# Ten short constant products in one tile ahead of the first hash bits, and the second pair's hash bits made by halves and signed in place

## The chip, the cores and the metric

The kernel runs on one core of a Trainium2 chip. The metric is device time in microseconds (us) of the whole program, as the median of repeated executions. A core has five engines that run their own instruction lists in order and wait for each other on semaphores: TensorE (PE in the profile, with PEld for its weight loads), VectorE (DVE), ScalarE (ACT), GpSimd (POOL) and SyncE (SP, which only issues DMAs here). ACT and POOL can issue DMAs too.

## The reference

The program computes a masked attention and then a feed-forward block on its output.

```python
# q, k, v: (4, 8, 768, 64); proj: (64, 6)
q_bits = (np.einsum('bhsd,dk->bhsk', q, proj) > 0)
k_bits = (np.einsum('bhsd,dk->bhsk', k, proj) > 0)
q_bucket = np.sum(q_bits * 2**np.arange(6), axis=-1)   # k_bucket likewise
mask = q_bucket[:, :, :, None] == k_bucket[:, :, None, :]
scores = np.where(mask, scale * q @ k.T, -1e9)
attn = softmax(scores)                                 # row maximum taken off first
x = (attn @ v) as (3072, 512)
h = x @ w_in;  g = h * erf(softplus(h));  out = g @ w_out   # w_in (512, 2048), w_out (2048, 512)
```

Six hash bits of every query and key row come from the signs of a projection; a query attends only to the keys with the same six bits.

## The kernel before, in words

**Pairs and scores.** The 32 heads are worked in 16 pairs; the two heads of a pair lie in the two halves of the 128 partitions (64 dimensions each). For a pair, q and k lie transposed as 128x768 f32. Scores are made transposed (keys on partitions, queries along the free dimension) in 12 chunks of 128 keys by 384 queries for both heads; `score(n, c)` (L550) makes one chunk, with n counting groups of three chunks, four groups per pair. A chunk is two products per head added up in PSUM: one of the f32 q and k, and one in bf16 of "bit tiles" that adds a very large negative number wherever the six bits differ. The bit tiles of a pair lie in `both[i % 2]`, a 128x2x768 bf16 tile (q in the first half, k in the second). ACT takes the exponential of every chunk (`e_all`, L568), and PE multiplies it with v (`av`, L631). DVE sums the exponentials for the divisor (L619), and PE adds them over partitions (`z_ps`, L666).

**Hash bits.** There are two ways to make them.

- By halves, in place (`hash_bits`, L373, and `take_bits`): four products of 64 output rows by 384 columns put the q bits on PSUM rows 0 to 63 and the k bits on rows 64 to 127; ACT writes the signs as bf16 straight into `both` (`sign_bits`, L386); DVE weights the k part onto both heads' partitions (`spread_bits`, L397) and copies the q part to the second head's partitions (`double_bits`, L407). The kernel before does this for pair 0 only, each half of 384 columns for itself, ahead of everything else.
- By way of DRAM (`bits_of`, L812; `sign_of`, L821; `weigh_bits`, L831; `leave_bits`, L841; `place_bits`, L850): four products of 32 output rows each, which PE runs side by side, make all bits of a pair in one 128x384 tile; ACT signs it into `sg`, DVE weights half of it, POOL sends it to DRAM (`bd`) and reads it back with two DMAs into the few rows of `both` that hold bits. The other rows must hold zeros, so each of the two `both` tiles is cleared once (a POOL memset: L433 for `both[1]` at the start, `clean`, L859, for `both[0]` after pair 0's last score). The kernel before does this for pairs 1 to 15.

**The start.** DVE sets a few constants. `WARM = 5` products of constant 128x128 and 128x256 f32 operands (L780) stand on PE ahead of pair 0's bits; each takes a new tile from a PSUM pool with one buffer (`bank`), so each waits for the one before it. Their operands lie in `w_sum`, which DVE sets first (L248). The first q and k are fetched in halves: SP issues q first half, k second half, q second half; ACT issues k first half. Then come v, pair 1, two pieces of w_in (`raw`) and pair 2, all on SP.

**What sets the order.** After the start, all steps of the attention are handed to a planner, `arrange`, as operations with an engine, an assumed cost, a rank, predecessors and a lateness; it emits them in an order, and that order is fixed per engine. PE's own order is written by hand (`order`): the scores of groups 0, 1, 2, then `bits_of(1)`, then `weigh` of groups 0 and 1, scores of groups 3 and 4, `bits_of(2)`, divisor 0, `weigh` of groups 2 and 3, and so on. Scores and bits share three PSUM buffers (`big`), so each waits for ACT to have read the one three places earlier. The first score of pair 1 is in group 4. Weights come as float64 bit patterns; POOL fetches them in pieces of 512 KB (`raw`, L456) with two buffers, and ACT and DVE turn them into f32 through the attention (L470 to L532). The feed-forward block follows on the same engines.

The lines that say how the five constant products are placed, and how the bits of pair 1 reach `both`:

```python
                nc.tensor.matmul(
                    out=bank("warm")[:, 0 : 2 * P],
                    lhsT=warm[:, 0:P],
                    rhs=warm[:, P:HS],
...
                nc.gpsimd.dma_start(out=bd.rearrange("n a r c -> (n a r) c"), in_=sg)
```

Of the kernel before, what the change touches and what calls it, by code (L numbers as in the profile page):

```python
# [63 lines left out]
P = 128  # L64
# [129 lines left out]
def kernel(  # L194
# [11 lines left out]
    nc = tc.nc  # L206
    B, H, S, D = v.shape
# [5 lines left out]
    HS = S // 2  # L213
# [15 lines left out]
    small = ctx.enter_context(tc.tile_pool(name="small", bufs=3))  # L229
    QR = 32  # L230
    QB = QR // 2
    WARM = 5
    proj_sb = const.tile([P, 2 * QR], F32, name="proj_sb")
    weight = const.tile([P, 2], F32, name="weight")
    proj_q = const.tile([P, QR], F32, name="proj_q")
# [9 lines left out]
    blocks = []  # L245
    stats = const.tile([P, 2, NPAIR, 2], F32, name="stats")
    nc.vector.memset(ones, 1.0)
    nc.vector.memset(w_sum[:, 0, 0, 0:HS], 1.0)  # L248
    warm = w_sum[:, 0, 0, 0:HS]
    proj_in = const.tile([P, 2 * NBIT], F32, name="proj_in")  # L250
    nc.gpsimd.dma_start(out=proj_in, in_=proj2)
    nc.vector.memset(proj_sb, 0.0)
# [46 lines left out]
    def bank(name):  # L299
        return misc.tile([P, 512], F32, name=name, tag="bank")  # L300
# [45 lines left out]
    def fetch(i, load, quick=False):  # L346
        d = dict(
            q=load.tile([P, S], F32, name="q", tag="q"),
            k=load.tile([P, S], F32, name="k", tag="k"),
            v=load.tile([P, NC, P], F32, name="v", tag="v"),  # L350
        )
        b, j = divmod(i, JP)
        parts = ((0, "q"), (0, "k"), (1, "k"), (1, "q")) if quick else ((None, "q"), (None, "k"))
        for half, what in parts:
            cols = slice(0, S) if half is None else slice(half * HS, half * HS + HS)
            queue = nc.scalar if quick and what == "k" and half == 0 else nc.sync
            for ab in range(2):
                queue.dma_start(
                    out=d[what][ab * D : ab * D + D, cols],
                    in_=qkT[2 * i + ab, "qk".index(what) * D : "qk".index(what) * D + D, cols],  # L360
                )
# [54 lines left out]
    def attention():  # L416
        NS = NPAIR * 4
        with (
# [11 lines left out]

            sg = bitp.tile([P, HS], BF16, name="sg")
            both = [bitp.tile([P, 2, S], BF16, name=f"both{n}") for n in range(2)]
            nc.gpsimd.memset(both[1], 0.0)  # L433
            junk = ep.tile([P, HS], BF16, name="junk")
            NE = 3 * GC
            e_all = ep.tile([P, NE, 2, HS + 1], F32, name="e_all")
# [339 lines left out]
                pairs[i] = fetch(i, load)  # L776

            pairs[0] = fetch(0, load, quick=True)
            for n in range(WARM):
                nc.tensor.matmul(  # L780
                    out=bank("warm")[:, 0 : 2 * P],
                    lhsT=warm[:, 0:P],
                    rhs=warm[:, P:HS],
                    start=True,
                    stop=True,
                )
# [11 lines left out]
            def pe(fn, args, cost, after=()):  # L798
                if chain:
                    after += (chain[-1],)  # L800
                op(fn, args, "PE", cost, (0, len(chain)), after, late=0.25)
                chain.append((fn.__name__,) + args)

            def bits_of(i):


                d = pairs[i]
                d["bits"] = big("bits")
                for n, what in enumerate("qk"):
                    for half in range(2):  # L810
                        row = (2 * n + half) * QR
                        nc.tensor.matmul(  # L812
                            out=d["bits"][row : row + QR, 0, 0:HS],
                            lhsT=proj_q,
                            rhs=d[what][:, half * HS : (half + 1) * HS],
                            start=True,
                            stop=True,
                        )
# [35 lines left out]
                        in_=bd[:, ab, 0 : NBIT + 1, :].rearrange("n r c -> r n c"),  # L854
                    )

            def clean():

                nc.gpsimd.memset(both[0], 0.0)  # L859

            chain = []
            order = [("score", 0)]
            for h in range(NH):
                order += [("score", n) for n in (2 * h + 1, 2 * h + 2) if n < NS]
                if h == 0:
                    order.insert(3, ("bits", 1))
                if h % 2 and (h + 3) // 2 < NPAIR:
                    order.append(("bits", (h + 3) // 2))
                if h >= 1:
                    order.append(("divisor", h - 1))  # L870
                order += [("weigh", 2 * h), ("weigh", 2 * h + 1)]
            slots = []
            for what, n in order:
                if what == "score":
                    i = n // 4
                    after = (("place_bits", i),)
                    if n == 0:
                        for c in range(2):
                            pe(plain, (n, c), 0.66)
                    for c in range(GC):  # L880
                        free = (slots[-3],) if len(slots) >= 3 else ()
                        pe(score, (n, c), 0.82 if n or c == 2 else 0.17, after + free)
                        slots.append(("exponential", n, c))
                elif what == "bits":
                    pe(bits_of, (n,), 0.92, (("start_pair", n), slots[-3]))
                    slots.append(("sign_of", n))
                elif what == "divisor":
                    pe(divisor, (n,), 0.42, (("sum_keys", n, last_sum(n)), ("keep_divisor", n - 1)))
                else:
                    h = n // 2  # L890
# [46 lines left out]
            for i in range(NPAIR):  # L937
                n = 4 * i
                if i:
                    op(  # L940
                        start_pair,
                        (i,),
                        "SP",
                        3.6,
                        (0, n - 6),
                        (("weigh", n - 9), ("bits_of", i - 1))
                        + tuple(("measure", i - 3, m, half) for m in range(2) for half in range(2)),
                        late=3.5,
                    )
                    op(sign_of, (i,), "ACT", 0.6, (0, n - 6, 9), (("bits_of", i), ("leave_bits", i - 1)))  # L950
                    op(weigh_bits, (i,), "DVE", 0.33, (0, n - 6, 1), (("sign_of", i),))
                    op(leave_bits, (i,), "POOL", 0.7, (0, n - 6, 2), (("weigh_bits", i),), late=2.6)
                    op(
                        place_bits,
                        (i,),
                        "POOL",
                        1.2,
                        (0, n - 6, 3),
                        (("leave_bits", i), ("score", n - 5, 2)) + (("clean",),) * (i == 2),
                        late=2.6,  # L960
                    )
                for m in range(2):
                    for half in range(2):
                        op(
                            measure,
                            (i, m, half),
                            "ACT",
                            0.5,
                            (1, 2 * i + 2, 2 + m, half),
                            (("start_pair", i), ("score", n, 0)),  # L970
                        )
                if i == NPAIR - 1:
                    continue
# [13 lines left out]
                op(normalise, (i,), "DVE", 0.95, (0, n + 8, 4), (("widen", i), ("leave", 2 * i + 1)))  # L987
                op(send, (i,), "SP", 0.35, (0, n, 4), (("normalise", i),), late=2.2)
            op(clean, (), "POOL", 1.4, (0, 0), (("score", 3, 2),), late=0.3)
            for n in range(len(pieces)):  # L990
                op(
                    fetch_weights,
# [771 lines left out]
```

## Time and profile before

| what | value |
|---|---|
| median of 17 runs | 919.82 us (918.64 to 922.63) |
| the profiled execution | 918.42 us, of which its span is 916.6 us |
| busy in the span | PE 904.6, DVE 819.7, ACT 767.9, POOL 46.5 us |
| attention, about | 10 to 320 us |
| feed-forward, about | 320 to 917 us |
| DMA | 83.05 MB, mean 91 GB/s |

The span runs from the first to the last instruction; all places below are microseconds from its start. The profiled execution is 1.8 us longer than its span, and 1.4 us shorter than the median. Busy time of PE counts a matmul from its start to its modelled end, so passes that overlap are merged. An f32 product shows as two records (two passes), a bf16 product as one. A releaser is what ended an engine's idle time.

### The profile page before, as it was taken

Reading aid. Unit: us, or ns where it says so; the run is one execution under the profiler, and the core shown is the slowest. Engines: PE = TensorE matmul, PEld = TensorE weight load, DVE = VectorE, ACT = ScalarE, POOL = GpSimd, SP = SyncE. Lnnn points to the kernel's source line nnn. Section 1 sums busy time; section 2 is a strip of 40 time slices with the busy share of each in tenths; the row PEclk is TensorE's granted clock in tenths of the full one; section 3 lists DMA queues with packets and bytes.
Section 4 is the critical chain, followed back from the end, with each engine's and each line's share of the span. In section 5 each row is a group of like instructions: output and inputs, shape, how many; then the busy total and the mean of one; then the engine's idle time right before and its main releaser. Section 6 shows DMA issues by size and latency. Waiting matters only on the chain.

```text
span 916.6 us, 13120 instructions
## 1 busy us (share of the span) xinstructions
PE 904.6 (99%) x5006; PEld 658.8 (72%) x5006; DVE 819.7 (89%) x1020; ACT 767.9 (84%) x1002; POOL 46.5 (5%) x83
## 2 busy tenths in 40 slices
PE   9999999999999999999999999999999999999997
PEld 4444444444444478888888888888888888888885
DVE  4899999999998979899999799988899889988995
ACT  5788887788887749999988998899989997899892
POOL 1211111111111000000000000000000000000000
PEclk9999999999999999999999999999999999999999
DMA  8455567655673131102022112201121121111201
GB/s 206 122 151 160 158 184 192 184 147 158 185 200 98 59 122 64 46 3 101 12 72 78 36 46 69 81 35 46 70 81 35 35 75 40 36 35 46 69 35 49
DMA packets 62966, 83.05 MB, mean 91 GB/s; under 512 B 34174, under 2 KB 47342, under 8 KB 62896
## 3 DMA queue, kind: packets, MB, share of 16 engines
q1 hardware_dynamic: 56672, 64.08, 24.2%
q0 software_dynamic: 6064, 17.86, 6.1%
q8 instruction: 41, 0.67, 0.3%
q14 instruction: 29, 0.24, 0.1%
q10 hardware_dynamic: 160, 0.20, 0.1%
HBM read 64.71 MB, written 17.40 MB: 90 GB/s over the span
## 4 chain that ended last, share of the span: by engine, by line
PE 96%; DVE 2%; ACT 1%; DMA 1%; issue 0%; POOL 0%; DVEq 0%; ACTq 0%; POOLq 0%
PE M L1323 31%; PE X L1183 28%; PE st L550 16%; PE av L631 14%; PE M L1183 3%; PE z_ps L666 1%; PE bits L812 1%; PE warm L780 1%; ACT e_all L568 1%; DVE e L1237 0%; DMA bd<-sg 0%; PE bits L373 0%; DVE h L1265 0%; DMA both<-bd 0%; DVE S L1280 0%
## 5 line engine op out<-in xcount | busy, mean ns | idle before, releaser
L1250 DVE SCALAR_TENSOR_TENSOR e<-w,e 128x1024 f32<-128x1024 f32 x144 | 173.4, 1220 | 5.8 <-ACT w L1246 3.0
L568 ACT ACTIVATE e_all<-st 128x768 f32<-128x768 f32 x192 | 151.1, 812 | 14.0 <-PE st L550 13.1
L1246 ACT ACTIVATE w<-w,cq 128x1024 f32<-128x1024 f32 x144 | 160.6, 1143 | 1.9
L550 PE MATMUL st<-q,k 64*128 64x384 f32 x768 | 155.2, 483 | 0.0
L1323 PE MATMUL M<-w_out_sb,h 128*128 128x256 f32 x576 | 140.2, 379 | 0.4 <-DVE h L1265 0.4
L631 PE MATMUL av<-e_all,v 128*64 128x385 f32 (+1 forms) x768 | 131.2, 490 | 0.0
L1183 PE MATMUL X<-x,w_in_sb 128*128 128x256 f32 x512 | 121.1, 379 | 0.0
L1323 PEld LDWEIGHTS M<-w_out_sb,h 128*128 128x128 f32 x576 | 109.3, 190 | 15.9 <-DVE h L1265 1.1
L1183 PEld LDWEIGHTS X<-x,w_in_sb 128*128 128x128 f32 x512 | 97.0, 190 | 13.8 <-ACT h L1201 0.6
L631 PEld LDWEIGHTS av<-e_all,v 128*64 128x64 f32 x768 | 52.3, 136 | 67.5 <-issue 66.6
L1323 PE MATMUL M<-wt,S 128*128 128x256 f32 x384 | 93.4, 379 | 0.4 <-DVE S L1280 0.4
L550 PEld LDWEIGHTS st<-q,k 64*128 64x128 f32 x768 | 68.3, 188 | 35.0 <-issue 34.3
L1183 PE MATMUL X<-x_sum,w_sum 128*128 128x256 f32 x344 | 81.7, 380 | 1.8 <-ACT h L1201 1.8
L1323 PEld LDWEIGHTS M<-wt,S 128*128 128x128 f32 x384 | 72.9, 190 | 10.7 <-DVE S L1280 0.8
L1183 PEld LDWEIGHTS X<-x_sum,w_sum 128*128 128x128 f32 x344 | 65.0, 190 | 12.0 <-ACT h L1201 3.3
L1201 ACT COPY h<-X 128x512 f32<-128x512 f32 x85 | 49.0, 576 | 22.3 <-PE X L1183 21.4
L1227 DVE SCALAR_TENSOR_TENSOR w<-w,e 128x1024 f32<-128x1024 f32 x48 | 58.4, 1221 | 9.7 <-ACT w L1222 9.6
L550 PE MATMUL st<-both 64*128 64x384 bf16 x384 | 63.1, 324 | 0.9 <-DMA both<-bd 0.9
L1265 DVE TENSOR_TENSOR h<-h,e 128x1024 f32<-128x1024 f32 x48 | 58.0, 1220 | 5.8 <-ACT e L1261 5.5
L1241 ACT ACTIVATE w<-e 128x1024 f32<-128x1024 f32 x48 | 50.4, 1050 | 13.3 <-DVE e L1237 13.0
L1237 DVE TENSOR_TENSOR e<-e,w 128x1024 f32<-128x1024 f32 x48 | 57.5, 1218 | 2.7 <-ACT e L1233 2.6
L1205 DVE TENSOR_TENSOR h<-X,h 128x512 f32<-128x512 f32 x65 | 44.8, 690 | 16.3 <-PE X L1183 15.4
(133 smaller groups left out, 1377.1 us busy)
## 6 DMA issues: line engine op xcount, KB each, us to landing
wt<-wt SPq DMA_DIRECT2D x24, 768.0 KB, 4.2
raw<-in_w_out_dram POOLq DMA_DIRECT2D x16, 512.0 KB, 4.0
raw<-in_w_in_dram POOLq DMA_DIRECT2D x14, 512.0 KB, 4.4
v<-in_v_dram SPq DMA_DIRECT2D x32, 192.0 KB, 4.7
xs<-x SPq DMA_DIRECT2D x16, 384.0 KB, 2.6
q<-in_qkT_dram SPq DMA_DIRECT2D x30, 192.0 KB, 4.1
k<-in_qkT_dram SPq DMA_DIRECT2D x30, 192.0 KB, 4.2
r<-rd SPq DMA_DIRECT2D x30, 192.0 KB, 3.4
```

Of the source, the lines that this page charges most:

```text
L550: nc.tensor.matmul(out=st[:, ab, 0:HS], lhsT=d["k" + src][rows, keys], rhs=d["q" + src][rows, cols], start=(part == 0), stop=(part == 1),)
L568: nc.scalar.activation(out=e[:, :, 0:HS], in_=st[:, :, 0:HS], func=AF.Exp, scale=scale)
L631: nc.tensor.matmul(out=d["av"][rows, 0:w], lhsT=d["v"][:, g * GC + c, rows], rhs=e[:, ab, 0:w], start=(g == 0 and c == 0), stop=(g == 1 an ...
L1183: nc.tensor.matmul(out=d[where][:, u, :], lhsT=a[:, kc, f : f + P], rhs=b[:, kc, :], start=(first and u == 0 and kc == 0), stop=(last and ...
L1201: nc.scalar.copy(out=quarter(p, q), in_=st[p][where])
L1227: nc.vector.scalar_tensor_tensor(out=w, in0=w, scalar=-1.0, in1=st[p]["e", v], op0=ALU.add, op1=ALU.subtract)
L1237: nc.vector.tensor_tensor(out=s, in0=s, in1=st[p].pop(("w", v)), op=ALU.subtract)
L1241: nc.scalar.activation(out=z, in_=st[p]["s", v], func=AF.Square)
L1246: nc.scalar.activation(out=q, in_=z, func=AF.Square, bias=cq[:, j : j + 1])
L1250: nc.vector.scalar_tensor_tensor(out=s, in0=st[p].pop(("q", v, j)), scalar=ERF_Q[j][1], in1=s, op0=ALU.add, op1=ALU.mult,)
L1265: nc.vector.tensor_tensor(out=h, in0=h, in1=st[p].pop(("s", v)), op=ALU.mult)
L1323: nc.tensor.matmul(out=banks[name][:, sub, :], lhsT=a[:, u, sub * P : (sub + 1) * P], rhs=b[:, u, :], start=(c == 0 and k == 0), stop=(c = ...
```

## The change

Four edits, and what they carry with them:

1. Ten constant products in place of five. All ten write one tile (`warm = bank("warm")`, taken once), rows 0 to 63, 128 columns; the weights are the 128x64 tile `ones`, the moving operand is one column of `ones` repeated 128 times. The memset of `w_sum` (L248) goes.
2. `bits_of(1)` calls `hash_bits`: four products of 64 rows by 384 columns. `place_first` (ACT) signs all 768 columns into `both[1]`, `weigh_first` (DVE, twice) and `double_first` (DVE) do the rest. `sign_of(1)`, `weigh_bits(1)`, `leave_bits(1)` and `place_bits(1)` go, and with them three DMAs on POOL. Scores of pair 1 wait for `double_first`.
3. The memset of `both[1]` at the start goes, since all of `both[1]` is now written; `clean` is there for both tiles, after the last score of pair 0 and of pair 1, ahead of pairs 2 and 3.
4. `leave_bits` and `place_bits` tell the planner a lateness of 3.6 in place of 2.6.

The order of instructions by engine differs only here. PE: the constant products and the bits of pair 1. DVE: the memset is gone; two `spread` and one `double` of 64x768 stand in the place of one 64x384 weighting; just after it, the read of `av`'s last column (`ev`) comes two instructions later, the two shifts of weight piece 1 come ahead of group 1's sums instead of after them, and the weighting of pair 2's bits one sum earlier. ACT: the sign of pair 1's bits comes one `junk` (a square with a sum) later, and one reading of a weight piece (`keep<-raw`) comes one exponential earlier. POOL: no memset at the start and no DMAs for pair 1, so `clean(0)` is first, then the weight piece; a second `clean` stands ahead of pair 3's DMAs. SP is unchanged, and so is everything after.

```diff
-    WARM = 5
+    WARM = 10
...
-    nc.vector.memset(w_sum[:, 0, 0, 0:HS], 1.0)
-    warm = w_sum[:, 0, 0, 0:HS]
...
-            nc.gpsimd.memset(both[1], 0.0)
...
+            warm = bank("warm")
             for n in range(WARM):
                 nc.tensor.matmul(
-                    out=bank("warm")[:, 0 : 2 * P],
-                    lhsT=warm[:, 0:P],
-                    rhs=warm[:, P:HS],
+                    out=warm[0:D, 0:P],
+                    lhsT=ones,
+                    rhs=ones[:, 0:1].broadcast_to([P, P]),
...
             def bits_of(i):
+                if i == 1:
+                    hash_bits(pairs[i], big)
+                    return
...
-            def clean():
-
-                nc.gpsimd.memset(both[0], 0.0)
+            def place_first():
+
+                cols = slice(0, S)
+                sign_bits(pairs[1], lambda what: both[1][:, "qk".index(what[0]), :], cols)
+
+            def weigh_first(ab):
+                spread_bits(pairs[1], slice(0, S), ab)
+
+            def double_first():
+                double_bits(pairs[1], slice(0, S))
+
+            def clean(n):
+
+                nc.gpsimd.memset(both[n], 0.0)
...
-                    after = (("place_bits", i),)
+                    after = (("double_first",) if i == 1 else ("place_bits", i),)
...
-                    pe(bits_of, (n,), 0.92, (("start_pair", n), slots[-3]))
-                    slots.append(("sign_of", n))
+                    pe(bits_of, (n,), 0.92 if n > 1 else 1.44, (("start_pair", n), slots[-3]))
+                    slots.append(("sign_of", n) if n > 1 else ("place_first",))
...
+                    if i == 1:
+                        op(place_first, (), "ACT", 0.9, (0, n - 2, 9), (("bits_of", i),))
+                        for ab in (1, 0):
+                            op(weigh_first, (ab,), "DVE", 0.43, (0, n - 2, 1), (("place_first",),))
+                        op(double_first, (), "DVE", 0.35, (0, n - 2, 2), (("weigh_first", 0), ("weigh_first", 1)))
...
-                        (("leave_bits", i), ("score", n - 5, 2)) + (("clean",),) * (i == 2),
-                        late=2.6,
+                            (("leave_bits", i), ("score", n - 5, 2), ("clean", i - 2)),
+                            late=3.6,
...
-            op(clean, (), "POOL", 1.4, (0, 0), (("score", 3, 2),), late=0.3)
+            for n in range(2):
+                op(clean, (n,), "POOL", 1.4, (0, 4 * n), (("score", 4 * n + 3, 2),), late=0.3)
```

More of the change, by code (lines that the diff above doesn't have):

```diff
@@ L865, in attention @@
                 if h == 0:
-                    order.insert(3, ("bits", 1))
+                    order.append(("bits", 1))
                 if h % 2 and (h + 3) // 2 < NPAIR:
@@ L949, in attention @@
                     )
[L950 to L958, printed above, removed]
-                        (("leave_bits", i), ("score", n - 5, 2)) + (("clean",),) * (i == 2),
-                        late=2.6,
-                    )
+                    if i == 1:
[3 more added lines that the diff above has]
+                        op(double_first, (), "DVE", 0.35, (0, n - 2, 2), (("weigh_first", 0), ("weigh_first", 1)))
+                    else:
+                        op(sign_of, (i,), "ACT", 0.6, (0, n - 6, 9), (("bits_of", i), ("leave_bits", i - 1)))
+                        op(weigh_bits, (i,), "DVE", 0.33, (0, n - 6, 1), (("sign_of", i),))
+                        op(leave_bits, (i,), "POOL", 0.7, (0, n - 6, 2), (("weigh_bits", i),), late=3.6)
+                        op(
+                            place_bits,
+                            (i,),
+                            "POOL",
+                            1.2,
+                            (0, n - 6, 3),
+                            (("leave_bits", i), ("score", n - 5, 2), ("clean", i - 2)),
+                            late=3.6,
+                        )
                 for m in range(2):
```

## The prediction

> **What bounds the kernel now.** The page first: its busy times, then its chain.
>
> ```profile
> PE 904.6 (99%) x5006; PEld 658.8 (72%) x5006; DVE 819.7 (89%) x1020; ACT 767.9 (84%) x1002; POOL 46.5 (5%) x83
> PE 96%; DVE 2%; ACT 1%; DMA 1%; issue 0%; POOL 0%; DVEq 0%; ACTq 0%; POOLq 0%
> ```
>
> TensorE sets the time almost everywhere, so a microsecond that PE gets back early is kept to the end unless another engine cannot follow. The change touches the first 50 us only, so I read the chain there, in order of time (start, duration, what):
>
> ```profile
> 1.40 1.24 PE warm L780 x2
> ...
> 7.74 2.54 PE bits L373 x8
> 10.27 1.70 PE st L550 x10
> 11.97 0.02 issue
> 11.99 5.14 ACT e_all L568 x8
> ...
> 20.24 2.72 DMA bd<-sg
> ...
> 24.21 2.15 DMA both<-bd
> 26.36 0.05 issue
> 26.40 2.59 PE st L550 x17
> 28.99 0.78 PE bits L812 x8
> ```
>
> Two things are seen. The constant products hold PE until 7.7 us. And at 20 to 26 us the chain is not PE's but runs through the two DMA hops of pair 1's bits. PE's timeline shows what that costs:
>
> ```profile
> 24.25 0.33 PE L550 MATMUL st<-both 64*128 64x384 bf16 x2
> 24.41 0.81 PE L550 MATMUL st<-q,k 64*128 64x384 f32 x4
> 25.88 0.32 PE L550 MATMUL st<-both 64*128 64x384 bf16 x1 [0.66 <-DMA both<-bd]
> 27.15 0.39 PE L550 MATMUL st<-both 64*128 64x384 bf16 x2
> ```
>
> Score chunks come every 0.80 to 0.81 us (22.62, 23.44, 24.25), so the next bit products were due at 25.06. The pair after them starts at 27.15 in place of 25.86: 1.29 us lost. For the start I read the weight loader's timeline, then SP's issues and their median from issue to landing:
>
> ```profile
> 2.67 0.50 PEld L780 LDWEIGHTS warm<-w_sum 128*128 128x128 f32 x2 [0.78 <-PE warm L780]
> 3.54 1.24 SPq L358 DMA_DIRECT2D q<-in_qkT_dram  x2
> q<-in_qkT_dram SPq DMA_DIRECT2D x4, 96.0 KB, 2.9
> ```
>
> Every constant product waits 0.78 us for the one before, at a pitch of 1.27. The last data that pair 0 needs is q's second half, whose second DMA is issued at about 4.2 (half of 1.24 after 3.54). It lands at about 6.8 to 7.1 (the k issues on ACT's queue take 2.6, these 2.9).
>
> Last, how much room DVE has in the attention (columns: stretch, length, busy PE, PEld, DVE, ACT, POOL, clock, DMA share, GB/s):
>
> ```profile
> 88.00:268.00 180.00, 180.00 (x1334) 83.60 (x1328) 171.04 (x228) 146.81 (x272) 26.02 (x46) 1.00 0.62 169
> ```
>
> PE is full, and DVE is at 95%: a second engine that can become the bound.
>
> **1. The constant products.** The `w_sum` memset goes. The first weight load stood 0.06 after that memset's end (1.34); `ones` is set at 0.93, so it now starts at 0.99. The old products took until 7.67, where bits begin. The new ones have no wait between them. Price of a pass: the 384-column f32 passes of pair 0's bits start at 7.67, 8.36, 9.00 and 9.64, 0.64 each, so 128 columns take 0.21 and twenty passes 4.3. With 0.1 for the first load PE is free at 5.4. Bounds: at the later pitch (f32 score passes, 0.32) 2.1 us; if each product kept a wait, the old pitch of 1.27 without half its columns (0.43), 0.84, times ten, 8.4. I take 4.3: these are passes in one queue without waits, as the bits are.
>
> **2. Pair 0's bits.** First half at 5.4: `proj_sb` is written by 4.3, and the first q and k land by 2.2 + 2.9 = 5.1. The second half waits for its q: 6.9 (middle of 6.8 and 7.1). Its two passes end at 7.55 with 0.32 each, where the first scores stood at 10.20: 2.65 earlier (2.45 to 2.75 by the landing). If passes still take 0.64 then, they end at 8.2. Late next is that DMA; the products no longer are. ACT's first sign took 0.58, DVE's first half 0.32 + 0.32 + 0.25. The first bit products come two chunks (1.3) after the scores' start, and the second half's DVE work is first needed by the score group after that, as before; all these shift together. ACT's exponentials follow PE from 11.99, then from 9.3.
>
> The clock. In this trace the 0.64 passes last until about 10.2, nine microseconds after the constant products began, with gaps, and two and a half after the gaps ended. The Trainium skill ("TensorE: Matmul & The Clock Gate", Part 1) states that the array runs at half rate until one window of about 3.4 us has been busy, the window running free of the kernel. By the rule ten gapless products from 1.0 release it by 7.8 at the latest, by the row alone possibly not before 9.9. The rule would leave the sum as it stands; staying slow to 9.9 is the second case below.
>
> **3. Pair 1's bits on PE.** Four 32-row products run side by side in 0.78 (the chain's last line). Two at a time at full rate take half of pair 0's 2.54: 1.27. Cost 0.49, on the path. Bounds: 0.4 to 0.6, from passes of 0.32 without and with a start gap of 0.1.
>
> **4. The way of the bits.** Gone are the sign of 0.58, the weighting of 0.32, three DMAs and two landings (2.7 and 2.2). New: ACT signs 128x768, between the 0.81 of an exponential of that size and twice 0.58; DVE runs two 64x768 weightings (0.32 to 0.64 each) and a copy (0.25 to 0.51). On the clock of before, bits end at 19.1; ACT has a `junk` pair in front (0.71) and is free at 19.85; sign to 20.7 (21.0); DVE to 22.3 (22.8). The score that needs it stands at 25.06 + 0.49 = 25.55: 2.7 us of cover at the worst. So the whole 1.29 is gained. Behind the new DVE work are two shifts of a weight piece (1.1) and, later than before, `ev` (end about 24.8); the product that waits for `ev` stands at about 29, and ACT's reading of `av` no longer waits for it. Group 1's sums start about 1.4 later than PE's pace asks; the exponentials that overwrite their input come at 35.09 before, with 4 us of cover left. What DVE is behind is made up by its own idle time (0.7 at 43.4, 0.6 at 62.4). Extra DVE work: 0.57 to 1.47 us, taken 1.2, at nothing. One cost I charge: ACT's reading of a weight piece (0.65) now stands before the third exponential of group 3, whose buffer PE wants 0.5 later: 0.15 (0 to 0.65).
>
> **5. The memsets and POOL.** The memset at 2.45 (1.40) had an idle POOL and delays nothing. `clean(0)` no longer stands behind two DMA issues (1.14) and starts with the last reading of `both[0]` (24.25 + 0.33). The weight fetch queued behind it came at 26.09; on the clock of before it now comes at about 26.9, when DVE is done with its buffer, which is 24.3 after the gain of 2.65. Landing takes 5.5, to 29.8, and ACT wants it at 35.80 - 3.3 = 32.5. `clean(1)` runs at about 46 on the old clock, between a weight fetch (43.30) and pair 3's DMA (51.82): nothing behind it waits. SP's queue is unchanged, and the fetch of pair 3 follows PE.
>
> The same memset beside DVE: `clean(0)` ran at 24.77 with a 1.75 us sum beside it, which took 1.75 elsewhere too. The Trainium skill ("SBUF — State Buffer", Who interferes with whom) states that a GpSimd instruction and a VectorE one in a two-port mode lock each other out for the whole instruction. By the row `clean(1)` costs nothing, by the rule up to 1.4 on DVE, which its idle time there covers; the sum goes by the row.
>
> **Sum** against the profiled execution (918.42 = span 916.6 + 1.8 around it): -2.65 - 1.29 + 0.49 + 0.15 = -3.3, so 915.1. The median of the 17 runs is 1.4 above this execution. I carry 1.2 of it, since a slow clock that lasts longer in other executions hurts before more than after: 916.3.
>
> **The rivals.**
>
> - *Forecast*, 916.3, chance 0.62.
> - *The clock stays slow until 9.9 as now* (for: the old products did not release it in six microseconds, and the new ones fill only 64 array columns; against: no gaps). Scores start at 8.2, 1.7 us of them at half rate lose 0.85: -2.0 + 0.85 - 1.29 + 0.49 + 0.15 = -1.8, 917.8. Chance 0.15.
> - *DVE takes the bound* (for: 95% busy; against: idle of 1.3 us by 62 and PE without a wait for DVE in the attention). Then its 1.2 and a blocked 1.4 come on top: -0.7, 918.9. Chance 0.10.
> - *A new wait takes the stall's place*: pair 1's scores wait for DVE behind something not counted, 1.29 given back: 917.6. Chance 0.07.
> - *Slower: ten products carry a fixed time each.* Place: before the first bits. With pitch p they end at 1.0 + 10p in place of 7.67; the rest gains 0.65. At 0.84 the time is 1.1 longer, 920.7; at 1.27 5.4 longer, 925. It is slower from p = 0.73, by over 0.2% from 0.92. The passes' 0.43 speaks against it. Chance 0.06.
>
> **How the numbers follow.** 0.2%, about 1.84 us, is what this kernel's measurement can tell from no change: faster is below 918.0, slower above 921.7. Faster: nearly all of the forecast (0.61), most of the second case (0.10), the new wait (0.06), some of DVE's (0.03): 0.80. Slower: the upper part of the last rival and what I do not see, 0.06. Same: 0.14. The range starts at the sum with its best bounds (-3.55: landing 6.8, no ACT cost) with nothing carried, 914.9, less a little for faster passes: 914.5. It ends at 918.6, which takes in the second case and the new wait.
>
> **What would show it.** Right: constant passes at 0.21 or less without gaps, ending by 5.5; bits' second half near 6.9; first scores near 7.55; no `st<-both` wait at pair 1; its bits 1.27 long; PE's later chunks 3.3 us earlier than now, all the way to the end. Wrong: passes of 0.64 after 8 us; a `DVE` releaser ahead of a score or of `av`; the lead of PE shrinking between 30 and 320 us.

## The result and the profile after

| what | before | after |
|---|---|---|
| median of runs | 920.03 us (918.36 to 922.63) | 916.62 us (915.41 to 916.86) |
| profiled execution | 918.42 us, span 916.6 | 915.52 us, span 913.6 |
| ratio of the runs' times, 95% interval | | 0.9961 [0.9953, 0.9969] |

The change makes the kernel 3.4 us faster by the medians; the forecast was 916.3. The whole interval lies beyond the 0.2% that the prediction called measurable.

The page of the kernel after, its busy times:

```profile
PE 902.5 (99%) x5016; PEld 660.7 (72%) x5016; DVE 820.8 (90%) x1021; ACT 768.0 (84%) x1002; POOL 45.0 (5%) x80
```

PE is as full as before (99%) and PE's busy time fell by 2.1 us, while DVE's rose by 1.1. PE's timeline of the kernel after (start, duration, instruction, in brackets the idle time before it and what ended it) shows where the time went:

```profile
0.99 4.53 PE L778 MATMUL warm<-ones 128*64 128x128 f32 x20 [0.99 <-DVE ones L247]
...
5.31 0.76 PE L371 MATMUL bits<-q,proj_sb 128*64 128x384 f32 x1
...
5.91 0.49 PE L371 MATMUL bits<-q,proj_sb 128*64 128x384 f32 x1
6.75 0.51 PE L371 MATMUL bits<-q,proj_sb 128*64 128x384 f32 x1 [0.36 <-DMA q<-in_qkT_dram]
...
7.10 0.49 PE L371 MATMUL bits<-q,proj_sb 128*64 128x384 f32 x1
...
7.64 1.56 PE L547 MATMUL st<-q,k 64*128 64x384 f32 x8
...
15.24 0.54 PE L371 MATMUL bits<-q,proj_sb 128*64 128x384 f32 x1
...
16.58 4.05 PE L628 MATMUL av<-e_all,v 128*64 128x385 f32 x24
...
22.19 0.33 PE L547 MATMUL st<-both 64*128 64x384 bf16 x2
...
23.00 0.33 PE L547 MATMUL st<-both 64*128 64x384 bf16 x2
...
61.25 0.33 PE L547 MATMUL st<-both 64*128 64x384 bf16 x2
...
62.39 0.34 PE L547 MATMUL st<-both 64*128 64x384 bf16 x2 [0.17 <-ACT e_all L565]
```

The same places in PE's timeline of the kernel before (first scores, pair 1's bits, pair 2's bits, and the two chunks near 61 us):

```profile
10.20 1.56 PE L550 MATMUL st<-q,k 64*128 64x384 f32 x8
...
17.81 0.52 PE L812 MATMUL bits<-q,proj_q 128*32 128x384 f32 x2
...
28.93 0.52 PE L812 MATMUL bits<-q,proj_q 128*32 128x384 f32 x2
...
64.66 0.33 PE L550 MATMUL st<-both 64*128 64x384 bf16 x2
...
65.57 0.34 PE L550 MATMUL st<-both 64*128 64x384 bf16 x2
```

From here on the *lead* of a kernel at some place is the start of an instruction in the profiled execution of before, less the start of the same instruction in that kernel. Read down the timeline, it is:

- **Start.** The twenty passes of the constant products run in one row and end at 5.52. The second half of the bits then waits 0.36 for q's second half, and the first scores start at 7.64 in place of 10.20: lead 2.56.
- **Pair 1's bits.** They take 1.34 (15.24 to 16.58) where before took 0.78 (17.81 to 18.59): lead 2.57 falls to 2.01.
- **The stall.** Chunks come at 22.19 and 23.00, the pace of 0.81, and no wait for `both` is left. Before lost its time here, so the lead grows: pair 2's bits stand at 25.52 against 28.93, lead 3.41.
- **A loss at 61 us.** The chunk after 61.25 was due at 62.06 (61.25 + 0.81) and starts at 62.39, behind a wait for ACT. Before has these two at 64.66 and 65.57, so the lead falls from 3.41 to 3.18. Nothing in the prediction spoke of this place.

After that the lead stays at 3.18 to 3.16 into the feed-forward, and the span is 3.0 shorter. What makes ACT late at 61 us is seen on POOL and ACT, in the timeline of the kernel after:

```profile
48.41 0.55 POOL L842 DMA_DIRECT2D bd<-sg  x1 [4.92 <-DVE sg L832]
54.33 1.15 POOL L851 DMA_DIRECT2D both<-bd  x2 [5.36 <-issue]
55.47 1.14 POOL L453 DMA_DIRECT2D raw<-in_w_in_dram  x2
59.82 0.68 ACT L467 ACTIVATE keep<-raw 128x512 f32<-128x512 f32 x1 [3.56 <-DMA raw<-in_w_in_dram]
```

and in that of the kernel before:

```profile
51.82 0.55 POOL L841 DMA_DIRECT2D bd<-sg  x1 [7.95 <-DVE sg L831]
57.32 1.14 POOL L850 DMA_DIRECT2D both<-bd  x2 [4.95 <-PE st L550]
58.45 1.14 POOL L456 DMA_DIRECT2D raw<-in_w_in_dram  x2
63.00 0.69 ACT L470 ACTIVATE keep<-raw 128x512 f32<-128x512 f32 x1 [3.32 <-DMA raw<-in_w_in_dram]
```

Pair 3's bits leave POOL 3.41 earlier than before (48.41, 51.82), as PE does. POOL then stands until they are in DRAM, reads them back, and only then fetches two weight pieces. (For this wait the timeline of after names `issue`, and that of before a score of PE that had long been done; where the fetches are moved, below, the profile names the DMA of the bits.) ACT takes the first piece in order, ahead of the next exponentials, so the piece's landing sets ACT's time. It comes only 3.18 earlier, and that is the lead which is left.

### The profile page after: what moved, and what is told of

It is laid out like the page before. It is cut to its first block, busy times and chain, and to the rows that moved or that the text cites. A ratio compares the mean times of both kernels' runs of the same rounds, so it can differ in the third digit from the quotient of the medians.

```text
span 913.6 us, 13138 instructions
## 1 busy us (share of the span) xinstructions
PE 902.5 (99%) x5016; PEld 660.7 (72%) x5016; DVE 820.8 (90%) x1021; ACT 768.0 (84%) x1002; POOL 45.0 (5%) x80
## 4 chain that ended last, share of the span: by engine, by line
PE 91%; DVE 2%; issue 1%; DMA 1%; ACT 0%; POOL 0%; DVEq 0%; POOLq 0%; ACTq 0%
PE M L1342 31%; PE X L1202 28%; PE st L547 14%; PE av L628 12%; PE M L1202 3%; PE z_ps L663 1%; PE bits L813 1%; DMA raw<-in_w_in_dram 0%; DVE e L1256 0%; DVE h L1284 0%; DVE S L1299 0%; DVE h L1224 0%; DVE x_sum L340 0%; DVE w L1246 0%; ACT h L1220 0%
```

## The experiments

### Each part alone

**The ten products alone**, on the kernel before:

```diff
-    WARM = 5
+    WARM = 10
-    nc.vector.memset(w_sum[:, 0, 0, 0:HS], 1.0)
-    warm = w_sum[:, 0, 0, 0:HS]
...
+            warm = bank("warm")
...
-                    out=bank("warm")[:, 0 : 2 * P],
-                    lhsT=warm[:, 0:P],
-                    rhs=warm[:, P:HS],
+                    out=warm[0:D, 0:P],
+                    lhsT=ones,
+                    rhs=ones[:, 0:1].broadcast_to([P, P]),
```

> The kernel before with the ten short products in one tile, and nothing else. Theory (the gains of the two edits stand apart): PE's first exponential comes 2.56 us earlier, as in the changed kernel, and the stall of about 1.3 us at pair 1's first scores stays; the time is 2.4 to 2.7 us below the kernel before, 917.5. Rival (pair 1's bits come by DMA at a time that PE's lead does not move, because pair 2's fetch fills the queues until 21.5 us): the stall grows to 2.5 us or more and the time is only 0.5 to 1.5 below.

Measured: 923.64 us, ratio 1.0045 [1.0032, 1.0058]: *slower* by 3.8, where both theories had it faster. The gain at the start is there (lead 2.37 at the scores), but past pair 1 the lead is -4.3. PE's and POOL's timeline of this kernel around the place:

```profile
17.87 0.55 POOL L840 DMA_DIRECT2D bd<-sg  x1 [14.02 <-DVE sg L830]
22.04 0.81 PE L548 MATMUL st<-q,k 64*128 64x384 f32 x4
24.59 1.14 POOL L849 DMA_DIRECT2D both<-bd  x2 [6.17 <-DMA bd<-sg]
28.10 0.48 PE L548 MATMUL st<-both 64*128 64x384 bf16 x1 [5.25 <-DMA both<-bd]
28.92 0.50 PE L548 MATMUL st<-both 64*128 64x384 bf16 x1 [0.34 <-DMA both<-bd]
...
30.36 0.65 PE L548 MATMUL st<-both 64*128 64x384 bf16 x2
...
31.96 0.65 PE L548 MATMUL st<-both 64*128 64x384 bf16 x2
```

The bits of pair 1 leave POOL at 17.87, 2.37 earlier than before (20.24), but their way through DRAM is much longer. The same DMA in the list of issues (KB, then us to landing), first of this kernel, then of the kernel before:

```profile
bd<-sg POOLq DMA_DIRECT2D x1, 96.0 KB, 6.0
```

```profile
bd<-sg POOLq DMA_DIRECT2D x1, 96.0 KB, 2.7
```

PE waits 5.25 and 0.34 where it waited 0.66 and 0.20, and then the chunks come at half the pace: 30.36 to 31.96, 1.60 where it was 0.80. The table by stretches says why (stretch, length, busy PE, PEld, DVE, ACT, POOL, then the granted clock, the DMA share and GB/s):

```profile
22.00:25.00 3.00, 0.85 (x8) 0.23 (x4) 2.93 (x4) 2.28 (x4) 0.41 (x1) 1.00 0.27 70
26.00:28.00 2.00, 0.00 (x0) 0.00 (x0) 1.54 (x2) 0.00 (x0) 1.62 (x2) 0.50 0.75 175
28.00:30.00 2.00, 1.56 (x6) 1.00 (x8) 0.00 (x0) 0.00 (x0) 0.00 (x0) 0.50 0.81 238
30.00:32.00 2.00, 2.00 (x10) 1.09 (x7) 0.00 (x0) 0.81 (x1) 0.00 (x0) 0.50 0.06 25
33.00:36.00 3.00, 3.00 (x28) 1.19 (x28) 1.15 (x3) 2.79 (x7) 0.57 (x1) 1.00 0.00 0
```

The granted clock went from 1.00 to 0.50 while PE stood, and came back between 32 and 33. So a wait of 5.3 us cost a stretch at half pace besides itself. Pair 2's bits start at 33.25 where they were due about 25.2 at the undisturbed pace (21.88 and the 3.33 that the kernel after takes from the same chunk, 22.19 to 25.52): 8.0 us, or 6.7 more than the kernel before loses at this place (lead 2.37 to -4.3).

**Why the way through DRAM got longer.** SP issues pair 2's fetch from about 11 to 14.4 in the kernel before and to 15.0 here, since SP's queue does not follow PE there. In the kernel before, the bits' write starts at 20.24, when that fetch is nearly through; here it starts at 17.87, in its middle. To test this, the same kernel with pair 2's fetch moved to POOL's queue, behind pair 1's read-back:

```diff
-                pairs[i] = fetch(i, load)
+                pairs[i] = fetch(i, load, behind=nc.gpsimd if i == 2 else None)
...
-            queue = nc.scalar if quick and what == "k" and half == 0 else nc.sync
+            queue = behind or (nc.scalar if quick and what == "k" and half == 0 else nc.sync)
...
-                        "SP",
+                        "SP" if i != 2 else "POOL",
...
+                        + ((("place_bits", 1),) if i == 2 else ())
```

> The products-alone kernel again, with pair 2's fetch (six DMAs, 1.15 MB) taken from SP's queue and issued on POOL's, behind pair 1's two reads of the bits. Theory (in the products-alone kernel pair 1's bits, sent at 17.9, stood in the DMA queues behind pair 2's fetch, which landed between 18.4 and 23.6): sent at about 17.9 again, the bits land in 2.5 to 3 us and POOL reads them back at about 21.5, in place of 24.6; PE's wait at pair 1's first scores falls from 5.3 to 2 us or less, and the clock is not lowered there. PE may wait later for pair 2's own data. Rival (the POOL DMA path itself is slow there, by its descriptors): the landing stays at 5 us or more with the queues empty.

Measured: one execution of 920.5 us, read by its trace. POOL's and PE's timeline:

```profile
18.09 0.55 POOL L840 DMA_DIRECT2D bd<-sg  x1 [14.24 <-DVE sg L830]
20.67 1.26 POOL L849 DMA_DIRECT2D both<-bd  x2 [2.04 <-DMA bd<-sg]
23.51 0.33 PE L548 MATMUL st<-both 64*128 64x384 bf16 x1 [0.28 <-DMA both<-bd]
29.57 0.86 PE L811 MATMUL bits<-k,proj_q 128*32 128x384 f32 x2 [2.70 <-DMA k<-in_qkT_dram]
```

The write leaves at nearly the same time (18.09) and POOL waits 2.04 for it in place of 6.17; PE waits 0.28 in place of 5.25. The way through DRAM is short when the fetch is gone, so the fetch was the cause. How it lengthens the write is not shown: in the products-alone kernel the DMA share is 0.18 or less from 21.5 to 24.0, and still POOL waits until 24.59. (The fetch itself is now late: pair 2's bits wait 2.70 for k.)

**The bits in place alone**: the kernel after with the five old constant products.

```diff
-    WARM = 10
+    WARM = 5
+    nc.vector.memset(w_sum[:, 0, 0, 0:HS], 1.0)
...
-                    out=warm[0:D, 0:P],
+                    out=bank("warm")[:, 0 : 2 * P],
...
```

> The changed kernel with the five old products put back (each in a tile of its own, with the memset of w_sum), so the bits of pair 1 alone are changed. Theory: the start is as before (first exponential at 12.0), the stall of 1.3 us is gone and the bits take 0.5 us more; 0.6 to 0.85 us below the kernel before, 919.3. Rival (exponentials set the pace behind pair 1's bits): no gain, 920.0.

Measured: 919.08 us, ratio 0.9988 [0.9975, 1.0001]. The interval just takes in no change; the trace shows the gain. The lead is -0.1 at the first scores, 0.75 ahead of 61 us and 0.86 behind it, as the stall's 1.3 less the longer bits would have it. The two parts alone therefore give +3.8 and -0.8 against their before, +3.0 added up; together they give -3.4. They are no sum: the first part pays only because the second takes away the way through DRAM.

### What it is in the products

**Shape or waits.** Five products of the old shape, but all into one tile:

```diff
-    WARM = 10
+    WARM = 5
+    nc.vector.memset(w_sum[:, 0, 0, 0:HS], 1.0)
+    warm = w_sum[:, 0, 0, 0:HS]
-            warm = bank("warm")
+            flat = bank("warm")
...
-                    out=warm[0:D, 0:P],
+                    out=flat[:, 0 : 2 * P],
```

> The changed kernel with five products of the old shape (128x128 by 256 columns), but all in one tile. Theory (the waits between products were the cost, not their shape or number): ten passes of 0.43 us from about 1.5 end by 5.8, the second half of pair 0's bits still starts with its q at 6.75, and the time is within 0.4 us of the changed kernel, 916.7. Rival (short, half-width products matter for themselves): first scores 1.5 us or more later, 918 or above.

Measured: 915.63 us, ratio 0.9958 [0.9946, 0.9971]. The products take 1.40 to 5.66 instead of 1.40 to 7.74, and the scores stand at 7.68 (7.64 after). The shape of the products makes no difference that these runs can tell.

And the reverse, ten small products with a new tile each:

```diff
-            warm = bank("warm")
...
-                    out=warm[0:D, 0:P],
+                    out=bank("warm")[0:D, 0:P],
```

> The changed kernel with a tile of its own for each of the ten short products, so each waits for the one before. Theory (the wait carries a fixed time, the old pitch of 1.27 less half of the old columns, 0.43): a pitch of 0.75 to 0.85, the products end at 8.5 to 9.5, first exponential 3 to 4 us later than in the changed kernel; 919.8 to 921. Rival (pitch falls with the columns, to 0.5 or less): they end by 6, and the time is that of the changed kernel within 0.4.

Measured: 919.59 us, ratio 0.9999 [0.9991, 1.0008]. What the trace says of the tile `warm` in this kernel:

```profile
L777 PE MATMUL warm<-ones x20: 421/447/476, 1.0 to 8.0; 128*64 128x128 f32 x20
  PE warm L777: 4.1, 9
```

Nine waits of the weight loader, 4.1 us together, each for the product before. The products end at 8.39, a pitch of 0.74, and the scores stand 0.49 later than before. That is the whole of the gain given back: the one tile is what the first edit is worth, not the ten, the 64 columns or the missing memset.

**Fewer and more products.** None, and twenty:

```diff
-    WARM = 10
+    WARM = 0
```

> The changed kernel without constant products. Theory (they serve to raise the clock before the data lands): the first half's bits start when q has landed, at about 5, passes last 0.64, the clock is raised only after a window of 3.4 us full of work, between 8.5 and 12, and first scores start near 8.1 at half rate: 1 to 2 us slower than the changed kernel, 917.7 to 918.7. Rival (they are not needed, the data is the limit): within 0.4 of the changed kernel.

```diff
-    WARM = 10
+    WARM = 20
```

> The changed kernel with twenty short products in place of ten. Theory (passes of 0.21 at half and 0.11 at full rate, nothing hides them behind the landing at 6.75): the clock rises at 4.5 to 6, forty passes end at 7.3 to 8, first exponential about 1.1 us later than in the changed kernel; 917.7. Rival (the second half of the bits waits for data anyway and takes the extra products in): no later than 0.3 us.

With none: 917.27 us, ratio 0.9971 [0.9957, 0.9986]. PE's timeline there begins the scores at half pace (eight passes in 2.93 where after takes 1.56) and finds the full pace at 11.7:

```profile
8.34 2.93 PE L547 MATMUL st<-q,k 64*128 64x384 f32 x8
...
11.66 0.81 PE L547 MATMUL st<-q,k 64*128 64x384 f32 x4
```

In its trace the lead after the start is 2.1 below that of after, and its span 2.4 longer, but the medians differ by only 0.65, or by 1.4 if each is taken against the runs of before beside it (917.27 is 2.04 below 919.31, 916.62 is 3.41 below 920.03). The profiled execution (917.89) was above this kernel's median, that of after (915.52) below its own. How much the ten products are worth over none is therefore between 0.65 and 2.4, and not settled. With twenty: 916.71 us, ratio 0.9968 [0.9954, 0.9982]. The products hold PE until 7.72 and the scores start at 8.95, 1.3 later than after, as the count of passes says. The time can still not be told from that of after. One reason is in its trace, which loses nothing at 61 us (see the table below): it keeps a lead of 2.2, where after keeps 3.18 in one profiled execution and 2.58 in another.

**The DMA that the bits wait for.** k's second half moved to ACT's queue, so that q's second half is issued sooner:

```diff
-            queue = nc.scalar if quick and what == "k" and half == 0 else nc.sync
+            queue = nc.scalar if quick and what == "k" else nc.sync
```

> The changed kernel with the second half of pair 0's k issued on ACT's queue, behind the first half, so that SP issues q's second half 1.3 us earlier. Theory (the issue of that q sets the start): it lands at 5.4 to 5.6, the second half's bits start right behind the first's, at about 6.0 to 6.2, first exponential 0.5 to 0.8 us earlier than in the changed kernel, 915.9; ACT's table load moves from 2.0 to 3.3 and hides. Rival (the transfers are limited by the DMA engines, not by issue): q lands within 0.3 of 6.7, and nothing is gained.

Measured: 915.92 us, ratio 0.9964 [0.9950, 0.9977], no different from after. PE's timeline:

```profile
5.31 0.87 PE L371 MATMUL bits<-q,proj_sb 128*64 128x384 f32 x1
...
5.97 0.85 PE L371 MATMUL bits<-q,proj_sb 128*64 128x384 f32 x1
...
6.78 0.56 PE L371 MATMUL bits<-q,proj_sb 128*64 128x384 f32 x1
...
7.66 1.56 PE L547 MATMUL st<-q,k 64*128 64x384 f32 x8
```

The wait for q is gone, yet the scores do not move (7.66): the products' end at 5.5 and a first half at half pace (0.66 a pass) now take PE to 6.78 by themselves. PE's own limit (6.78) and that of the DMA (6.75 in the kernel after) stand within 0.1 us of each other. This run does not tell when q landed; the kernel with all edits together (below) does, and there the rival holds.

### The loss at 61 us

**The kernel after once more**, beside the next two:

> The changed kernel once more, beside the next kernels on one chip. Theory: 916.6 again, 3 to 3.6 us below the kernel before; the profile loses 0.2 to 0.8 of PE's lead near 61 us, where ACT waits for a weight piece.

Measured: 916.8 us, ratio 0.9970 [0.9959, 0.9981]. Here the loss is larger: the lead falls from 3.29 to 2.58, with ACT getting its piece at 60.41. Across the kernels that make pair 1's bits in place and leave the fetches where after has them, the lateness of that piece gives the loss almost to the hundredth. "Late" is the piece's start on ACT less where before has it (63.00) moved by the lead just ahead:

| kernel | lead ahead | piece on ACT | late by | lead lost |
|---|---|---|---|---|
| after | 3.41 | 59.82 | 0.23 | 0.23 |
| after once more | 3.29 | 60.41 | 0.70 | 0.71 |
| old shape, one tile | 3.37 | 60.23 | 0.60 | 0.61 |
| k's second half on ACT | 3.38 | 60.38 | 0.76 | 0.76 |
| ten products with waits | 0.35 | 63.43 | 0.78 | 0.78 |
| no products | 1.26 | 62.21 | 0.47 | 0.48 |
| twenty products | 2.10 | 60.12 | -0.78 | -0.12 |
| bits in place alone | 0.75 | 61.86 | -0.39 | -0.11 |
| without `clean(0)` (below) | 3.31 | 60.56 | 0.87 | 0.87 |

The lateness does not grow with the lead (0.78 at a lead of 0.35, 0.23 at 3.41), so it is not a time that stands still while PE gets earlier. Two landings ahead of it vary instead: POOL waits between 3.49 (twenty products) and 5.75 us (k's second half on ACT) for the bits, and the piece comes 4.35 (after) to 5.67 us (old shape) after its fetch is begun. In the kernel without `clean(0)` the bits themselves also left POOL 0.8 later (49.33) than its lead would have it. By its own pace of 0.81, PE loses 0.33 to 0.97 at this place in seven of these nine traces and nothing in two; in the three traces with pair 1's bits by way of DRAM it loses 0.10 (before), 0.18 (the products alone) and nothing (the later fetch). These are too few to say how much of the loss the change itself brings. Where the piece is early, the lead gains a little only, since PE itself had lost only 0.1 there in the kernel before (65.57 where 64.66 + 0.81 = 65.47 was due).

**The two fetches ahead of the read-back on POOL**, so that they do not wait for the bits:

```diff
-                            (("leave_bits", i), ("score", n - 5, 2), ("clean", i - 2)),
+                            (("leave_bits", i), ("score", n - 5, 2), ("clean", i - 2))
+                            + tuple(("fetch_weights", m) for m in (5, 6) if i == 3),
```

> The changed kernel with the two weight fetches on POOL put ahead of pair 3's two reads of its bits (which are not needed until about 70 us). Theory (the lead lost near 61 us is POOL standing in wait for pair 3's bits to land in DRAM, with the weight fetch queued behind): the fetch is issued at about 53.5 in place of 55.5, ACT's wait of 3.6 us before that piece shrinks to 1.6 or less, the lead of 3.4 us is kept to the end; 0.2 to 0.6 below the changed kernel. Rival (the loss comes from elsewhere): the lead still falls near 61 us, same time.

Measured: 915.32 us, ratio 0.9960 [0.9947, 0.9974]. POOL's and ACT's timeline of this kernel:

```profile
48.46 0.55 POOL L842 DMA_DIRECT2D bd<-sg  x1 [4.92 <-DVE sg L832]
49.19 0.53 POOL L453 DMA_DIRECT2D raw<-in_w_in_dram  x1 [0.17 <-issue]
53.38 0.53 POOL L453 DMA_DIRECT2D raw<-in_w_in_dram  x1 [3.67 <-ACT e_all L565]
54.55 1.15 POOL L851 DMA_DIRECT2D both<-bd  x2 [0.64 <-DMA bd<-sg]
56.21 0.70 ACT L467 ACTIVATE keep<-raw 128x512 f32<-128x512 f32 x1
```

The piece is there when ACT comes to it, with no wait; the read-back is issued no later than it was (54.55, against 54.63 in the run of after beside it). The lead goes through this place unhurt (3.35 ahead, 3.46 behind) and is 3.42 at the last products: the place and the cause are shown. In time it is 1.5 us below the kernel after beside it, 0.9984; resampling the runs of the two gives an interval of 0.9981 to 1.0000, so a gain is likely and its size, more than the 0.2 to 0.6 expected, is not settled. It is the lowest median measured here; by ratio the five old products in one tile (0.9958) are as low.

**All together**: this, with k's second half on ACT and nine products.

```diff
-    WARM = 10
+    WARM = 9
...
-            queue = nc.scalar if quick and what == "k" and half == 0 else nc.sync
+            queue = nc.scalar if quick and what == "k" else nc.sync
```

> The same with nine short products in place of ten and the second half of pair 0's k on ACT's queue. Theory (products, first half of the bits and landing are now all within 0.5 us of each other): first exponential 0.2 to 0.5 us earlier than in the changed kernel, 915.7 to 916.0. Rival (the clock, raised 0.5 us later by chance, takes it back): no difference from the kernel with the fetches moved alone.

Measured: 915.95 us, ratio 0.9960 [0.9940, 0.9979], the same as without the two further edits. Scores at 7.62, lead 2.58, and nothing is lost at 61 us. The first exponential was to come 0.2 to 0.5 earlier; the scores are only 0.02 earlier than in the profiled execution of after. The start has nothing more to give by these means: the second DMA of q's second half is issued at 2.92 in place of 4.2, but lands at 6.60, 3.68 later, and the bits wait 0.51 for it, to 6.74 (6.75 in after). So an earlier issue did not bring an earlier landing; why, is not shown.

### The memset beside DVE

In the kernel after, `clean(0)` runs beside one of DVE's shifts; the timeline of POOL and DVE:

```profile
22.64 1.38 POOL L871 MEMSET both<- 128x1536 bf16 x1 [20.17 <-PE st L547]
23.06 1.24 DVE L481 TENSOR_SCALAR top<-raw 128x512 int32<-128x512 int32 x1
```

The same instruction took 0.43 for the piece before (19.16). Without `clean(0)`:

```diff
-            for n in range(2):
+            for n in range(1, 2):
```

> The changed kernel without the clearing of both[0]; left out is that clearing, so the even pairs from 2 on read old rows and the scores of those pairs are other than the reference's. Theory (the shift of a weight piece on DVE took 1.24 us in place of 0.43 because POOL's memset ran beside it): it takes 0.43, DVE is 0.8 us ahead there, and the time does not change, since PE's lead behind it was 3.41 already. Rival (something else lengthened it): 1.2 us again.

Measured: one execution of 916.14 us. DVE's timeline:

```profile
23.17 0.43 DVE L481 TENSOR_SCALAR top<-raw 128x512 int32<-128x512 int32 x1
```

So the memset costs DVE 0.81. PE's lead is 3.31 behind it, no better than in the kernel after (3.41): the 0.81 does not reach PE. The loss at 61 us is there as well (3.31 to 2.44).

## Why the prediction was right, point by point

By the terms of its sum, profiled execution against profiled execution (-3.3 predicted, -2.9 measured):

- **Products, 4.3 for twenty passes, free at 5.4.** They ended at 5.52. Right, and the reason as well: the single tile, not the shape (five old products in one tile do as well; ten with waits give all back). The 0.78 that the prediction read as each product's wait is the weight loader's; PE itself got back 0.42 a product (a pitch of 1.27 with waits, 4.26 / 5 = 0.85 in one tile). The rival's price also holds, though its pitch was measured at 0.74 and not 0.84: it made the change slower from a pitch of 0.73, and at 0.74 the time was that of before (0.9999).
- **The start, -2.65.** -2.56. q's second half let the bits go at 6.75 in place of 6.9 (the middle of its two bounds is 6.95), and the passes then took 0.35. That they no longer ran at half rate was the choice against the second case, and by the first scores it held in every trace with products in one tile.
- **The stall, -1.29, and no new wait.** -1.35 (the lead from 2.06 to 3.41). ACT's sign took 0.90, the two weightings 0.86 and the copy 0.35: DVE was done at 19.1 on its own clock, and the score that needs it stood at 23.0. The cover was there as worked out.
- **Pair 1's bits on PE, +0.49.** +0.56, inside its bounds.
- **ACT's reading ahead of an exponential, +0.15.** Not seen: one exponential came late, and the lead was back at 3.41 behind it.
- **The 1.2 carried from the profiled execution to the median.** 1.1 (916.62 less 915.52). The reason given for it, a slow clock that lasts longer in other executions, was not tested.

**The step that failed** is "nothing behind it waits", said of POOL around pair 3's DMA, and with it the sentence that the lead, once gained, is kept. The weight pieces are queued behind pair 3's read-back, and the read-back behind the bits' landing. ACT takes a piece in order, and the lead lost 0.2 to 0.9 there in seven of nine traces (table above); two had no loss. The prediction followed the queue to `clean(1)` at 46 and the DMA at 51.82 and stopped one instruction too early: the wait of 4.95 and the two fetches at 58.45 stood in the trace of before, with ACT's wait of 3.32 at 63.00 behind them. By luck it was small enough (0.23 in the profiled run) for the ACT term, which did not come, to cover most of it; in the second profiled execution of the same kernel it was 0.71.

**Right in the sum, wrong as a sum.** The two gains were added as if each could be had alone. The products alone cost 3.8. The prediction named the wait through the two DMA hops, but not that a PE which is 2.4 earlier sends those bits into a fetch that is not earlier. For the change as a whole this had no part in the time, since both were made at once.

**The memset.** What the prediction said of `clean(1)` came true: it runs at 42.11 beside a sum of two inputs that takes 1.76 (41.99), as such sums do elsewhere. It did not ask the same of `clean(0)`, whose new place (22.64) stands beside a shift of one input. The Trainium skill ("SBUF — State Buffer", Who interferes with whom) states that VectorE instructions such as `tensor_scalar`, in a two-port mode, and GpSimd's lock each other out for the whole instruction. The runs agree: the shift took 1.24 beside the memset and 0.43 without it, and ended 0.28 after the memset's end (24.30, 24.02); that this shift runs in such a mode, no row says. PE's lead did not follow.

## What to carry to other kernels

A microsecond gained ahead of a DMA hop was kept here only where the hop moved along: look up what else is on the DMA engines at the *new* time, and which fetches do not follow the engine that got earlier. Follow every queue past the moved step until an instruction is found that has idle time in front of it, and read what that idle time waits for; here a place with a wait of several microseconds just off the critical path was where part of a gain ended. For the filler products of this kernel, a shared output tile was worth more than their number or shape.

## What the runs showed of the hardware that I had not expected

- **A short idle time of PE is paid twice.** After 5.3 us without a product, the granted clock was at 0.50 for about 7 us (0.89 on average between 25 and 26, 0.70 between 32 and 33); the wait of 2.7 us for pair 2's k, in the kernel with the later fetch, put it to 0.50 from 30 to 32 as well (0.59 on average between 29 and 30). The Trainium skill ("TensorE: Matmul & The Clock Gate", Part 1) states that the clock is lowered after at least one idle window of about 3.4 us and released after a busy one, the window running free of the kernel. Being released about 4.5 us after the next product agrees with that. Being lowered about 2.9 us after the last product in the first case, and about 2.3 in the second, does not: the second wait is shorter than a whole window.
- **What counts as busy at the start.** With products that wait for one another, the passes kept the half pace until about 10 us (0.64 for 384 columns in the kernel before and in the one with ten waits), though the records count PE as nine tenths busy or more from 3 us on. With products in one row, passes stood 0.32 to 0.39 apart from a place between about 5 and 7 us that differed from run to run; for the same five products in one tile it was 0.37 already at 5.6. The granted clock in the profile's rows is 1.00 in all of these stretches: at the start of this kernel it has to be read from the distance of the passes.
- **A small write behind a large fetch.** 96 KB from POOL landed in 2.7 us with the fetch of pair 2 nearly through (before), in 1.9 with that fetch moved, and in 6.0 beside it (the products alone).
